# Four transposes moved from TensorE to SP's queue, half steps in two more blocks, and one tile's preparation moved ahead

## The chip, the core and the metric

The kernel runs on one core of one Trainium2 chip. The time is device microseconds of one execution of the whole program. Before the change it is 333.25 us, the median of 3 runs (333.15 to 333.43). Times on the trace are counted in us from the start of the profiled span.

## The reference

An attention with a linear kernel, followed by a gated feed-forward layer with a norm in front:

```python
# q, k, v: 8 batches, 8 heads, 576 rows, 64 columns
r = np.maximum(x, 0.0)                       # for q and k
phi = np.concatenate([r * c, r * s], axis=-1)   # c, s: cos and sin of the row's angle
kv = np.einsum('bhsf,bhsd->bhfd', k_p, v)
z = np.sum(k_p, axis=2)
num = np.einsum('bhsf,bhfd->bhsd', q_p, kv)
den = np.einsum('bhsf,bhf->bhs', q_p, z)[..., None] + 1e-06
x = (num / den)                              # as 4608 rows of 512
xn = x / np.sqrt(np.mean(x * x, axis=-1, keepdims=True) + 1e-06) * rms_g
g = xn @ w_gate                              # 512 x 1536
out = (g * (1.0 / (1.0 + np.exp(-g))) * (xn @ w_val)) @ w_out   # 1536 x 512
```

## The kernel before

**Batches, tiles, blocks.** A batch of 576 rows is cut into four tiles of 128 rows, (b, 0) to (b, 3), and a fifth of 64 rows; the fifths of two batches make one tile (b, 4). The four tiles of a batch are the four column groups of one block of the feed-forward layer, so blocks 0 to 7 belong to batches 0 to 7, and block 8 holds the four tiles of fifths.

**One tile's way into a block.** Features of q (q_feat, L222 on ScalarE, ACT, or L224 on VectorE, DVE) are transposed to rqT, over SP's DMA queue (q_turn, L293) or on TensorE, PE (q_turn_pe, L304, and a copy out of PSUM in q_evict, L312 on DVE or L314 on ACT). num_mm (L326) multiplies rqT with kvm into a PSUM tile "att". divide (L352, L355, L364, on DVE) makes x from it. sumsq (L375 on ACT) sums the squares, and the power of -0.5 is taken on GpSimd (L380). norm (L385 on DVE) makes xn, one of three buffers. xn is then transposed into its column group of the block's operand xnT in one of two ways: x_turn (L393), one DMA transpose of 128 x 512 on SP's queue straight into xnT; or x_turn_pe (L403), four PE transposes into a PSUM tile "xps", and x_evict, a copy from there into xnT (L409 on DVE, L411 on ACT).

**Steps.** Each of the nine blocks has 12 steps, numbered through from 0 to 107, so block 1 starts with step 12, block 2 with 24, block 3 with 36 and block 4 with 48. A step makes a tile gps of PSUM (x times w_gate), a tile vps (x times w_val), the silu of gps (sil, L657, ACT) and the product of vps and sil (hT, L666, DVE). From block 2 on, each step also runs four matmuls of the output layer of the block before (acc, L465), whose sums ACT copies to osb (L471) for the stores to out on SP (L455). Between blocks 0 and 1 stands lead(), which prepares batch 1 while the output layer of block 0 runs.

Blocks 0 to 4 start before all four column groups of their operand are ready. For them the table PARTS says which columns a step takes (gv_mm_part, L433): T[0] to T[3] are the single tiles of 128 columns, T[4] is the first half (tiles 0 and 1), T[5] the second half (tiles 2 and 3). A step of a single tile does four row groups n with 4 x 4 = 16 matmuls of 128 columns for gps and as many for vps; a step of a half does two with 8 matmuls of 256 columns each. From block 5 on, a step is 4 + 4 matmuls of 512 columns (L420).

**Order.** The order on each engine is the program's order. A plan written by hand, at(step, place, function, arguments), puts the preparation into the steps. In a step the places run as follows: "sp", "act0", "dve0"; then the DMA transposes that x_turn_late has put on a list; then the matmuls of gps; "mid" (in blocks with PARTS); those of vps; silu; "act1"; "act2"; "dve1"; hT; acc; "pe". So "mid" stands on PE between gps and vps, "dve1" on DVE ahead of the step's hT, and "act0" on ACT ahead of its silu. tile_at puts a tile into three steps, with its transpose on SP two steps after num_mm; pe_tile_at does the same with the transpose on PE.

**Buffers in PSUM.** gps, vps, xps and the transposes of q share one pool of three buffers (tag "gv"); which of the three a tile gets, and so which reader it waits for, is settled when the program is built. att has two buffers of its own, acc one.

Of the kernel before, what the change touches and what calls it, by code (L numbers as in the profile page):

```python
# [17 lines left out]
def kernel(  # L18
# [20 lines left out]
    NNT = DFF // P  # L39
# [439 lines left out]
    def at(g, w, f, *a):  # L479
        plan[g, w].append(lambda: f(*a))  # L480
# [6 lines left out]
    def tile_at(g, key, xblk, col):  # L487
        at(g, "pe", num_mm, key)
        at(g + 1, "dve0", divide, key)
        at(g + 1, "act1", sumsq, key)  # L490
        at(g + 2, "dve0", norm, key)
        at(g + 2, "sp", x_turn_late, key, xblk, col)
# [29 lines left out]
    at(1, "act0", q_evict, 0, 3)  # L522
    at(1, "mid", x_turn_pe, (0, 2))
    at(1, "dve1", x_evict, (0, 2), 0, 2, True)
    at(1, "pe", num_mm, (0, 3))
    at(2, "dve0", divide, (0, 3))
    at(2, "act1", sumsq, (0, 3))
    at(3, "dve0", norm, (0, 3))
    at(4, "mid", x_turn_pe, (0, 3))
    at(4, "dve1", x_evict, (0, 3), 0, 3, True)  # L530
    for c in range(2):
        at(2 + c, "act2", q_feat, 0, J, c, True)

# [8 lines left out]
    def pe_tile_at(g, key, xblk, col, gx, first="act1"):  # L542

        at(g, "pe", num_mm, key)
        at(g + 1, "dve0", divide, key)
        at(g + 1, "act1", sumsq, key)
        at(gx, "dve0", norm, key)
        at(gx, "pe", x_turn_pe, key)
        at(gx + 1, first, x_evict, key, xblk, col)

    def q2_at(g, b, t):
        for c in range(2):
            at(g, "act2" if c else "dve1", q_feat, b, t, c, c == 1)
        if t < J:
            at(g, "pe", q_turn, b, t)
# [4 lines left out]
    at(12, "pe", num_mm, (1, 3))  # L560
    at(13, "dve0", divide, (1, 3))
    at(13, "act1", sumsq, (1, 3))
    for t in (2, 3):
        at(12 + t, "dve0", norm, (1, t))
        at(12 + t, "pe", x_turn_pe, (1, t))
        at(13 + t, "act1", x_evict, (1, t), 1, t)
    q2_at(12, 1, J)


# [7 lines left out]
    for t, g in enumerate((13, 19, 20, 21, 23)):  # L577
        q2_at(g, 2, t)
    pe_tile_at(22, (2, 1), 2, 1, 24)
    pe_tile_at(24, (2, 2), 2, 2, 26)  # L580
    pe_tile_at(25, (2, 3), 2, 3, 27)


    at(15, "pe", load_q, 3)
# [35 lines left out]
    def run(g, w):  # L620
# [4 lines left out]
    T = [(c * P, P) for c in range(J)] + [(hf * HB, HB) for hf in range(2)]  # L625
    PARTS = {0: tuple((n,) + T[c] for n, c in (
        (0, 0), (0, 1), (0, 2), (4, 4), (6, 4), (0, 3), (4, 5), (6, 5), (8, 4), (10, 4), (8, 5),
        (10, 5),
    ))}
    for blk in (1, 2, 3, 4):  # L630
        PARTS[blk] = tuple(
            [(n,) + T[c] for c in range(2) for n in (0, 4, 8)]
            + [(n,) + T[5] for n in range(0, NNT, 2)]
        )

    def step(blk, nn):
        g = blk * NNT + nn
        run(g, "sp")
        run(g, "act0")
        run(g, "dve0")  # L640
        while late_turns:
            x_turn(*late_turns.pop(0))
        if nn == 0:
            hT[blk] = htp.tile([P, NNT, TB], BF16, name="hT", tag="hT")
        if blk in PARTS:
            n0, c0, cn = PARTS[blk][nn]
            ni = TB // cn
            gp = gv_mm_part(wg, "gps", blk, n0, c0, cn)
            run(g, "mid")
            vp = gv_mm_part(wv, "vps", blk, n0, c0, cn)  # L650
            dst = hT[blk][:, n0 : n0 + ni, c0 : c0 + cn]
        else:
            gp = gv_mm(wg, "gps", blk, nn)
            vp = gv_mm(wv, "vps", blk, nn)
            dst = hT[blk][:, nn, :]
        sil = silp.tile([P, TB], BF16, name="sil", tag="sil")
        K(nc.scalar.activation(out=sil[:, :], in_=gp[:, :], func=AF.Silu))  # L657
        run(g, "act1")
        ends = blk > 1 and nn % 3 == 2
        if not ends:  # L660
            run(g, "act2")
        run(g, "dve1")
        a, c = vp[:, :], sil[:, :]
        if blk in PARTS:
            a, c = (z.rearrange("p (i n) -> p i n", i=ni) for z in (a, c))
        K(nc.vector.tensor_tensor(out=dst, in0=a, in1=c, op=ALU.mult))  # L666
        if blk > 1:
            for i in range(4 * nn, 4 * nn + 4):
                out_mm(blk - 1, i)
        if ends:  # L670
            run(g, "act2")
        run(g, "pe")
# [165 lines left out]
```

## Time and profile before

| | before |
|---|---|
| median of 3 runs | 333.25 us |
| the profiled execution | 333.33 us |
| its span, first to last instruction | 331.2 us |
| PE busy, of the span | 320.0 us |
| clock granted to PE, mean | 0.998 of full |
| DMA transposes of rqT / xnT on SP | 32 / 24 |
| PE transposes of xn | 12 tiles of 4 |

How to read the rows: in a timeline a row has the start and the duration in us, the engine, the line, the operation with what it writes and reads (out<-in), its shape and how many of them were merged; square brackets hold the idle time of the engine ahead of it and what ended it. The ends of matmuls are modelled and overlap the next ones, so the distance from one row's start to the next is the time that counts. A row of waits has the total in us, how often, and the longest. SPq is the queue of DMAs that SyncE issues; the duration there is that of issuing, and the time to landing is counted from the start of the issue. A landing row gives the fastest, the median and the slowest of the transfers asked for.

### The profile page before, as it was taken

The page shows a single profiled execution, that of the slowest core. Times are in us where ns is not written, and L with a number is a line of the kernel's source. Part 1 is how long each engine was busy: PE and PEld are TensorE (multiplying, and loading weights), DVE is VectorE, ACT ScalarE, POOL GpSimd, SP SyncE. Part 2 cuts the span into 40 slices and gives each one's busy share as a digit, 9 for nine tenths or more (in the row PEclk, how much of TensorE's full clock was granted, in tenths as well). Part 3 has the DMA queues.
Part 4 walks back from the last instruction along what each step waited for, and adds up shares of the span by engine and source line. Part 5 has one row for each costly group of instructions (what it writes and reads, how often), then busy time and mean ns, then how long its engine had stood idle before and what let it go on. Part 6 is the DMA issues. An engine that isn't in the chain of part 4 may idle for free.

```text
span 331.2 us, 7596 instructions
## 1 busy us (share of the span) xinstructions
PE 320.0 (97%) x3048; PEld 214.2 (65%) x3048; DVE 189.6 (57%) x393; ACT 169.7 (51%) x322; POOL 43.2 (13%) x84
## 2 busy tenths in 40 slices
PE   6789999999999999999999999999999999999995
PEld 5568866999887788778877744554444444444443
DVE  4675476877956585687867676756543422223200
ACT  3765377767864366575646564644432322332221
POOL 3743343200101000011110001000100000000000
PEclk9999999999999999999999999999999999999999
DMA  7999999994148999999699995245124020000012
GB/s 218 303 207 207 290 337 385 360 180 95 35 97 228 353 247 281 201 313 149 162 221 245 214 239 131 70 93 111 48 67 109 32 65 33 32 34 32 32 64 96
DMA packets 78019, 54.76 MB, mean 165 GB/s; under 512 B 49024, under 2 KB 71312, under 8 KB 77984
## 3 DMA queue, kind: packets, MB, share of 16 engines
q1 hardware_dynamic: 70704, 39.99, 48.7%
q0 software_dynamic: 7120, 14.16, 16.7%
q8 instruction: 24, 0.39, 0.5%
q10 hardware_dynamic: 160, 0.13, 0.1%
q14 instruction: 11, 0.09, 0.1%
HBM read 38.01 MB, written 9.44 MB: 143 GB/s over the span
## 4 chain that ended last, share of the span: by engine, by line
PE 92%; ACT 2%; DMA 2%; DVE 1%; issue 1%; SPq 0%; ACTq 0%; DVEq 0%
PE acc L465 27%; PE gps L433 16%; PE vps L433 16%; PE vps L420 13%; PE gps L420 13%; PE att L326 3%; PE att L269 3%; DMA kbuf<-in_k_dram 2%; PE xps L403 1%; PE qtp L304 1%; ACT kp L222 1%; DMA out_dram<-osb 1%; DVE xn L385 0%; ACT qp L222 0%; ACT xnT L411 0%
## 5 line engine op out<-in xcount | busy, mean ns | idle before, releaser
L666 DVE TENSOR_TENSOR hT<-vps,sil 128x512 bf16<-128x512 f32 x108 | 74.6, 691 | 98.3 <-PE vps L420 62.0
L657 ACT ACTIVATE sil<-gps 128x512 bf16<-128x512 f32 x108 | 64.3, 596 | 99.5 <-PE gps L420 60.1
L465 PE MATMUL acc<-wo,hT 128*128 128x512 bf16 x420 | 105.7, 379 | 0.0
L465 PEld LDWEIGHTS <-hT 128*128 128x128 bf16 x420 | 40.1, 98 | 39.7
L433 PE MATMUL gps<-xnT,wg 128*128 128x128 bf16 (+1 forms) x704 | 62.7, 238 | 0.8 <-DVE xnT L409 0.5
L433 PE MATMUL vps<-xnT,wv 128*128 128x128 bf16 (+1 forms) x704 | 62.8, 238 | 0.6 <-ACT sil L657 0.5
L433 PEld LDWEIGHTS <-wg 128*128 128x128 bf16 x704 | 50.3, 98 | 7.1 <-issue 0.8
L433 PEld LDWEIGHTS <-wv 128*128 128x128 bf16 x704 | 51.2, 98 | 3.8 <-issue 0.6
L380 POOL TENSOR_TENSOR rs<-ss,mhalf 128x1 f32<-128x1 f32 x36 | 20.4, 566 | 200.3 <-ACT sq L375 200.3
L420 PE MATMUL vps<-xnT,wv 128*128 128x512 bf16 x144 | 37.0, 379 | 0.0
L420 PE MATMUL gps<-xnT,wg 128*128 128x512 bf16 x144 | 36.9, 379 | 0.0
L471 ACT COPY osb<-acc 128x512 f32<-128x512 f32 x35 | 20.4, 584 | 31.5 <-PE acc L465 31.5
L420 PEld LDWEIGHTS <-wv 128*128 128x128 bf16 x192 | 18.8, 98 | 22.6
L385 DVE SCALAR_TENSOR_TENSOR xn<-x,rs,gb 128x512 bf16<-128x512 f32 x36 | 27.0, 749 | 7.9 <-POOL rs L380 7.6
L420 PEld LDWEIGHTS <-wg 128*128 128x128 bf16 x192 | 18.0, 98 | 20.1
L375 ACT ACTIVATE sq<-x 128x513 f32<-128x513 f32 x36 | 22.6, 628 | 7.6 <-DVE x L364 7.2
L364 DVE TENSOR_TENSOR x<-att,rec 128x512 f32<-128x512 f32 x36 | 24.9, 691 | 1.2
L224 DVE TENSOR_SCALAR kp<-kbuf,trig 128x512 bf16<-128x512 f32 x50 | 22.6, 483 | 3.5 <-DMA kbuf<-in_k_dram 3.1
L224 DVE TENSOR_SCALAR qp<-qbuf,trig 128x512 bf16<-128x512 f32 x50 | 22.9, 479 | 0.0
L222 ACT ACTIVATE kp<-kbuf,trig 128x512 bf16<-128x512 f32 x30 | 20.7, 714 | 2.8 <-DMA kbuf<-in_k_dram 2.8
L222 ACT ACTIVATE qp<-qbuf,trig 128x512 bf16<-128x512 f32 x30 | 21.1, 713 | 0.2 <-DMA qbuf<-in_q_dram 0.2
L326 PEld LDWEIGHTS <-rqT 128*128 128x128 bf16 x320 | 14.4, 98 | 7.9 <-DVE rqT L312 0.9
(64 smaller groups left out, 189.2 us busy)
## 6 DMA issues: line engine op xcount, KB each, us to landing
out_dram<-osb SPq DMA_DIRECT2D x70, 128.0 KB, 2.1
kbuf<-in_k_dram SPq DMA_DIRECT2D x5, 640.0 KB, 6.0
vbuf<-in_v_dram SPq DMA_DIRECT2D x5, 640.0 KB, 7.2
qbuf<-in_q_dram SPq DMA_DIRECT2D x5, 640.0 KB, 7.4
kbuf<-in_k_dram SPq DMA_DIRECT2D x5, 512.0 KB, 4.8
vbuf<-in_v_dram SPq DMA_DIRECT2D x5, 512.0 KB, 5.8
qbuf<-in_q_dram SPq DMA_DIRECT2D x5, 512.0 KB, 6.1
kbuf<-in_k_dram POOLq DMA_DIRECT2D x3, 640.0 KB, 10.4
```

Source lines behind the costliest of these rows:

```text
L222: K(nc.scalar.activation(out=dst, in_=src, func=AF.Relu, scale=scale))
L224: K(nc.vector.tensor_scalar(out=dst, in0=src, scalar1=scale, scalar2=0.0, op0=ALU.mult, op1=ALU.max,))
L326: K(nc.tensor.matmul(nums[key][:, h // Z, (h % Z) * E : (h % Z) * E + D + 1], lhsT=rqT[a, t][:, h, :], rhs=kvm[a % NK][:, h, 0 : D + 1], s ...
L364: K(nc.vector.tensor_tensor(out=x[:, 0:DM].rearrange("p (z s d) -> p z s d", z=2, d=D), in0=a[:, :, :, 0:D], in1=r.unsqueeze(3).to_broadca ...
L375: K(nc.scalar.activation(out=sq[:, :], in_=xs[key][:, :], func=AF.Square, scale=1.0 / math.sqrt(DM), accum_out=ss[:, :],))
L380: K(nc.gpsimd.tensor_tensor(out=rs[:, :], in0=ss[:, :], in1=mhalf[:, :], op=ALU.pow))
L385: K(nc.vector.scalar_tensor_tensor(out=xn[:, :], in0=xs.pop(key)[:, 0:DM], scalar=rss.pop(key)[:, :], in1=gb[:, :], op0=ALU.mult, op1=ALU. ...
L420: K(nc.tensor.matmul(ps[:, :], lhsT=w[:, dt, nn * P : (nn + 1) * P], rhs=xnT[blk][:, dt, :], start=(dt == 0), stop=(dt == NDT - 1),))
L433: K(nc.tensor.matmul(ps[:, i * cn : (i + 1) * cn], lhsT=w[:, dt, (n0 + i) * P : (n0 + i + 1) * P], rhs=xnT[blk][:, dt, c0 : c0 + cn], star ...
L465: K(nc.tensor.matmul(acc[blk][:, :], lhsT=hT[blk][:, nn, jt * P : (jt + 1) * P], rhs=wo[:, nn, :], start=(nn == 0), stop=(nn == NNT - 1),))
L657: K(nc.scalar.activation(out=sil[:, :], in_=gp[:, :], func=AF.Silu))
L666: K(nc.vector.tensor_tensor(out=dst, in0=a, in1=c, op=ALU.mult))
```

## The change

```diff
     at(1, "act0", q_evict, 0, 3)
     at(1, "mid", x_turn_pe, (0, 2))
     at(1, "dve1", x_evict, (0, 2), 0, 2, True)
-    at(1, "pe", num_mm, (0, 3))
-    at(2, "dve0", divide, (0, 3))
-    at(2, "act1", sumsq, (0, 3))
+    at(1, "mid", num_mm, (0, 3))
+    at(1, "dve1", divide, (0, 3))
+    at(2, "act0", sumsq, (0, 3))
     at(3, "dve0", norm, (0, 3))
-    at(4, "mid", x_turn_pe, (0, 3))
-    at(4, "dve1", x_evict, (0, 3), 0, 3, True)
+    at(3, "pe", x_turn_pe, (0, 3))
+    at(4, "dve0", x_evict, (0, 3), 0, 3, True)
...
-    for t in (2, 3):
-        at(12 + t, "dve0", norm, (1, t))
-        at(12 + t, "pe", x_turn_pe, (1, t))
-        at(13 + t, "act1", x_evict, (1, t), 1, t)
+    for t, g in ((2, 13), (3, 15)):
+        at(g, "dve0", norm, (1, t))
+        at(g, "sp", x_turn_late, (1, t), 1, t)
...
-    pe_tile_at(24, (2, 2), 2, 2, 26)
-    pe_tile_at(25, (2, 3), 2, 3, 27)
+    for t in (2, 3):
+        tile_at(22 + t, (2, t), 2, t)
...
     for blk in (1, 2, 3, 4):
-        PARTS[blk] = tuple(
-            [(n,) + T[c] for c in range(2) for n in (0, 4, 8)]
-            + [(n,) + T[5] for n in range(0, NNT, 2)]
-        )
+        head = (
+            [(n,) + T[c] for c in range(2) for n in (0, 4, 8)] if blk < 3
+            else [(n,) + T[4] for n in range(0, NNT, 2)]
+        )
+        PARTS[blk] = tuple(head + [(n,) + T[5] for n in range(0, NNT, 2)])
```

In block 0 the fourth tile's num_mm goes from the end of step 1 to between gps and vps of that step, its division ahead of hT of step 1, its sum of squares ahead of the silu of step 2, its PE transposes from between gps and vps of step 4 to the end of step 3, and the copy out of PSUM ahead of that of hT of step 4. Tiles (1, 2), (1, 3), (2, 2) and (2, 3) are transposed by one DMA each on SP's queue; their 16 PE transposes and 4 ACT copies go. The norm of (1, 2) is one step earlier, in step 13; that of (1, 3) stays in step 15, and those of batch 2 in steps 26 and 27. In blocks 3 and 4, the first six steps take tiles 0 and 1 together, 256 columns at a time, so tile 1 is wanted in the first step of the block and no longer in the fourth.

## Prediction

> **What bounds the kernel now.** I read the page first, then who waited for whom, then TensorE (PE) in order of time.
>
> ```profile
> span 331.2 us, 7596 instructions
> PE 320.0 (97%) x3048; PEld 214.2 (65%) x3048; DVE 189.6 (57%) x393; ACT 169.7 (51%) x322; POOL 43.2 (13%) x84
> PE 92%; ACT 2%; DMA 2%; DVE 1%; issue 1%; SPq 0%; ACTq 0%; DVEq 0%
> PE vps L433 <- ACT sil L657: 0.5, 1, 0.5
> ```
>
> PE is busy for 97% of the span and carries 92% of the chain that ended last. An edit therefore counts in one of three ways: it takes instructions off PE, it removes a wait of PE, or it gives PE a new one. The last row is such a wait, once, 0.5 us. PE has only nine kinds of waits in all, none longer than 0.6 us behind its start, so a shift is not swallowed further on: gains and losses add up.
>
> **Fourth tile of the first batch (block 0).** The wait lies in step 4:
>
> ```profile
> 28.55 1.04 PE L433 MATMUL gps<-xnT,wg 128*128 128x256 bf16 x8
> 29.42 0.39 PE L403 MATMUL xps<-ident_b,xn 128*128 128x128 bf16 x4
> 30.33 1.03 PE L433 MATMUL vps<-xnT,wv 128*128 128x256 bf16 x8 [0.52 <-ACT sil L657]
> 29.68 0.60 ACT L657 ACTIVATE sil<-gps 128x512 bf16<-128x512 f32 x1 [0.40 <-PE gps L433]
> ```
>
> Three PSUM buffers are shared by gps, vps and the transposes' xps. Here vps got the buffer of its own step's gps and had to wait until the silu (29.68 to 30.28) had read it. Without that it would have followed the four transposes, which cost 0.22 (rows below), at 29.65: 0.68 us lost. In the changed program as built, the transposes stand at the end of step 3 and step 4's vps waits for the hT product of step 3 instead. What has to be in time for that:
>
> ```profile
> 22.60 1.02 ACT L314 COPY rqT<-qtp 128x1024 bf16<-128x1024 bf16 x1
> 23.86 1.06 PE L433 MATMUL vps<-xnT,wv 128*128 128x128 bf16 x16
> 26.06 0.69 DVE L364 TENSOR_TENSOR x<-att,rec 128x512 f32<-128x512 f32 x1
> 26.85 0.63 ACT L375 ACTIVATE sq<-x 128x513 f32<-128x513 f32 x1
> 28.25 0.75 DVE L385 SCALAR_TENSOR_TENSOR xn<-x,rs,gb 128x512 bf16<-128x512 f32 x1 [0.49 <-POOL rs L380]
> ```
>
> The num matmuls now stand where vps stood (23.86), and their operand is there at 23.62, so they do not wait. The division goes ahead of hT of step 1 and ends near 25.5 instead of 26.75 (estimate); the sum of squares goes ahead of the silu of step 2, near 25.6. From sum to norm took 28.25 - 26.85 = 1.40, so the norm could start at 27.0; VectorE (DVE) is then in hT of step 2 and the norm follows at about 27.7, ending at 28.4, just before PE wants it at 28.55. The silu and hT that are pushed back have over 0.3 us of room. Gain between 0 (norm late, the wait merely moves) and 0.68; I take 0.68, because each row leaves it room.
>
> **Two tiles of block 1 (steps 13 to 18).**
>
> ```profile
> 62.70 1.06 PE L433 MATMUL gps<-xnT,wg 128*128 128x128 bf16 x16
> 64.48 0.39 PE L403 MATMUL xps<-ident_b,xn 128*128 128x128 bf16 x4
> 64.70 1.06 PE L433 MATMUL gps<-xnT,wg 128*128 128x128 bf16 x16
> 65.60 1.06 PE L433 MATMUL vps<-xnT,wv 128*128 128x128 bf16 x16
> 66.49 0.39 PE L403 MATMUL xps<-ident_b,xn 128*128 128x128 bf16 x4
> 66.92 1.05 PE L433 MATMUL gps<-xnT,wg 128*128 128x128 bf16 x16
> 70.49 1.04 PE L433 MATMUL gps<-xnT,wg 128*128 128x256 bf16 x8
> 64.01 0.57 ACT L657 ACTIVATE sil<-gps 128x512 bf16<-128x512 f32 x1
> 65.80 0.60 ACT L657 ACTIVATE sil<-gps 128x512 bf16<-128x512 f32 x1 [0.60 <-PE gps L433]
> ```
>
> Four transposes hold PE for 64.70 - 64.48 = 0.22 us; the second set costs 0.43, since the step behind it also waits 0.21 for a copy. From 62.70 (step 14) to 70.49 (step 18) are 7.79 us: four steps of 1.79, plus 0.22, plus 0.43. That 0.65 goes. But without the transposes the PSUM buffers fall differently. In the changed program as built, gps of step 15 waits for the silu of step 14, and vps of step 15 for the silu of its own step: block 0's wait moves here. The first silu ends at 64.58, so gps starts at 64.63 instead of 64.48: 0.15. Then gps runs 0.90, its silu starts 0.20 behind it (65.80 against 65.60), takes 0.60, and vps follows 0.05 later: 0.85 lost. Steps 14 to 17 take 7.16 + 1.00 = 8.16, 0.37 more than before, and step 18 wants its operand at 70.86, less the 0.68 of block 0: 70.18.
>
> Now the transposes as transfers. SP issues xnT of (1,2), then rqT of batch 2, then xnT of (1,3), then q of batch 3. Queued behind them are only rqT, wanted in step 19, and q, wanted from step 24.
>
> ```profile
> 63.57 0.74 DVE L385 SCALAR_TENSOR_TENSOR xn<-x,rs,gb 128x512 bf16<-128x512 f32 x1
> 65.36 0.74 DVE L385 SCALAR_TENSOR_TENSOR xn<-x,rs,gb 128x512 bf16<-128x512 f32 x1
> 64.13 1.34 SPq L293 DMA_TRANSPOSE rqT<-qp  x1
> DMA to landing us min/median/max: 6.3/6.3/6.3
> DMA to landing us min/median/max: 2.4/3.8/7.6
> ```
>
> The first landing row is this rqT alone, the second all 24 transfers of L393. The norm of (1,2) moves from 63.57 to the end of the division before it, ahead of hT of step 13; that hT is then about 0.7 later and is wanted only by gps of step 16. The norm of (1,3) stays in step 15 and ends at 65.36 + 0.74, less 0.68, at 65.42; SP is free by then, so this transfer starts at 65.45. Fastest (2.4) it lands at 67.85, and PE does not wait; slowest (7.6) at 73.05, and PE waits 2.9. The nearest row is the rqT directly ahead of it on the queue: it landed at 70.43 in the old trace, with the loads of batch 3 in flight. For transposes close behind each other:
>
> ```profile
> 146.26 1.63 SPq L293 DMA_TRANSPOSE rqT<-qp  x1
> 147.98 1.26 SPq L393 DMA_TRANSPOSE xnT<-xn  x1
> DMA to landing us min/median/max: 6.1/6.1/6.1
> DMA to landing us min/median/max: 4.8/4.8/4.8
> ```
>
> These land at 152.36 and 152.78, 0.42 apart. So I take 70.43 + 0.4 = 70.8 and a wait of 0.6 us at step 18. The Trainium skill, page "DMA: Bandwidth & Descriptors", section "Queues, rings and completion order", has each DMA engine consume one queue's descriptors in ring order; the 0.42 between these two landings agrees.
>
> The Trainium skill, page "VectorE: DVE Perf Modes", section "Rules for kernel authors", speaks against this part: TensorE for a 128x128 transpose where PSUM will do, the DMA crossbar otherwise. By the 390 ns of its section "The three transpose paths", the four removed sets would be worth an estimated 6.2 us of PE instead of 0.9; the trace has 0.22 a set, and the rows decide.
>
> **Two tiles of block 2.** Their transposes leave the ends of steps 26 and 27: 2 x 0.22 = 0.44. Built, the order of buffers brings no own-step wait here. The transfers are issued in steps 26 and 27 and wanted in step 30.
>
> ```profile
> 93.07 0.75 DVE L385 SCALAR_TENSOR_TENSOR xn<-x,rs,gb 128x512 bf16<-128x512 f32 x1 [0.17 <-POOL rs L380]
> 101.75 1.04 PE L433 MATMUL gps<-xnT,wg 128*128 128x256 bf16 x8
> ```
>
> The second tile's norm ends at 93.82; step 30 starts 7.9 later, 7.5 without the transposes. Between them on SP stand two stores of out, and behind them two rqT that are wanted in steps 32 and 34. At 3.8 the wait is nothing, at 7.6 with the stores ahead about 1; I take nothing. The four ScalarE copies that go are on no chain of PE, save the 0.21 counted above.
>
> **Half steps in blocks 3 and 4.** Twelve steps go from 2 x 16 matmuls of 128 columns to 2 x 8 of 256.
>
> ```profile
> 32.98 1.04 PE L433 MATMUL gps<-xnT,wg 128*128 128x256 bf16 x8
> 43.46 1.89 PE L465 MATMUL acc<-wo,hT 128*128 128x512 bf16 x8
> 118.17 1.06 PE L433 MATMUL gps<-xnT,wg 128*128 128x128 bf16 x16
> 119.96 1.03 PE L465 MATMUL acc<-wo,hT 128*128 128x512 bf16 x4
> 108.39 2.45 SPq L393 DMA_TRANSPOSE xnT<-xn  x1
> DMA to landing us min/median/max: 6.9/6.9/6.9
> 153.52 1.06 PE L433 MATMUL gps<-xnT,wg 128*128 128x128 bf16 x16
> ```
>
> Twelve runs of 8 fill 32.98 to 43.46, 0.873 each; two runs of 16 fill 118.17 to 119.96, 0.895 each. So 24 x 0.022 = 0.53 us. The price: the second tile of each block is now wanted in its first step, not its fourth. For block 3 it lands at 108.39 + 6.9 = 115.3 and is wanted at 118.17. For block 4 it lands at 152.78 and is wanted at 153.52, 0.74 of cover; both ends are set by PE's steps and move together. Nothing, then; with 7.6 instead of 4.8 it would be 2.1.
>
> **Sum.** 0.68 - 0.37 - 0.6 + 0.44 + 0.53 = 0.68 us off. The profiled execution took 333.33 (its span 331.2 and 2.1 around it), 0.08 over the median of 333.25; so 332.65 and 332.57. Forecast 332.6.
>
> **Rivals.**
> B, the transfer is hidden: (1,3) lands within 4.7 us of its issue, so step 18 does not wait. For it: the median of 3.8, and q now queues behind it. Against it: the 6.3 of its neighbour. Gain 1.28: 332.0. The Trainium skill, page "Advanced Engine Details and Errata", section "X-Bar Transpose (TRN2)", calls transpose DMAs as fast as regular ones, and by that rule B would hold; here the same kind of transfer took 2.4 to 7.6.
> C, slower: three transposes among plain loads make (1,3) land late. All gains are gone at 6.0 us from issue, and at 7.6 the net is 1.6 lost: 334.8; between the two about 334.2. For it: 6.9 and 7.6 do occur beside loads. Against it: the median of 3.8, and that q's loads now start behind it. It is slower by more than 0.2% from 6.7 us on.
> D, the second tile of block 4 is late in step 48, by 2.1 at most: 334.6. Against it: the cover of 0.74.
> E, it does not do what it says: the norm of the fourth tile is late, and the 0.68 is not won: 333.2.
>
> **How the numbers follow.** Forecast 0.40, B 0.28, C 0.20, D 0.07, E 0.05. A measurement of this kernel can tell about 0.2% (0.67 us) from no change; the forecast sits on that bound and gives half of its chance to each side. Faster: 0.20 + 0.28 = 0.48. Slower: 0.14 of C and 0.06 of D, 0.20. Within: 0.32. Range 331.9 (B, a little under) to 334.4 (C up to a wait of 2.4); the likeliest case alone is 332.0 to 333.1.
>
> **What would show it.** Step 4's vps starts as gps ends; a wait for sil of about 0.85 stands before vps in step 15; a wait for xnT stands before gps in step 18, 0 to 1.2; the runs of x16 in blocks 3 and 4 are gone, 0.02 a run; no transposes at the ends of steps 14, 15, 26, 27. Wrong would be: no wait in step 15, over 1.3 in step 18, any wait in step 30, 36 or 48.

## The result and the profile after

The changed kernel takes 332.82 us (median of 22 runs, 332.6 to 333.21), the kernel before 333.39 (22 runs beside them, 333.06 to 333.69). The ratio is 0.9985, with a 95% interval of 0.9978 to 0.9991: 0.57 us off between the medians, where 0.68 was forecast. The interval leaves out 1, so the gain is clear of the noise of these runs; it is under the 0.2% (0.67 us) that the prediction set as its bound, and by that bound it falls under no change. The profiled execution took 332.82 with a span of 330.7.

The page of the changed kernel, its span and the busy times of the engines:

```profile
span 330.7 us, 7188 instructions
PE 319.5 (97%) x2840; PEld 211.1 (64%) x2840; DVE 189.5 (57%) x393; ACT 167.8 (51%) x318; POOL 42.8 (13%) x84
```

From the view of who waited for whom, the waits of PE that are new or have moved (total, times, longest):

```profile
PE vps L433 <- ACT sil L657: 0.7, 1, 0.7
...
PE gps L433 <- DMA xnT<-xn: 0.5, 1, 0.5
...
PE acc L465 <- ACT osb L471: 0.2, 1, 0.2
```

PE issues 208 fewer matmuls (3048 to 2840). Sixteen of them are the transposes; the other 192 come from the half steps, where one matmul of 256 columns takes the place of two of 128 and saves only 0.02 us a run of 8. The three waits are where gains went: one for a silu (0.5 us, in another place, before), one for a DMA transpose, and one for a copy to osb.

Where they stand, on PE's timeline (start, duration, idle before and its cause). Steps 3 and 4 of block 0 first, then steps 12 and 14 to 18 of block 1:

```profile
28.47 0.39 PE L403 MATMUL xps<-ident_b,xn 128*128 128x128 bf16 x4
28.69 1.04 PE L433 MATMUL gps<-xnT,wg 128*128 128x256 bf16 x8
29.56 1.04 PE L433 MATMUL vps<-xnT,wv 128*128 128x256 bf16 x8
...
58.20 1.05 PE L433 MATMUL gps<-xnT,wg 128*128 128x128 bf16 x16
...
62.03 1.06 PE L433 MATMUL gps<-xnT,wg 128*128 128x128 bf16 x16
62.92 1.06 PE L433 MATMUL vps<-xnT,wv 128*128 128x128 bf16 x16
63.97 1.05 PE L433 MATMUL gps<-xnT,wg 128*128 128x128 bf16 x16
65.71 1.05 PE L433 MATMUL vps<-xnT,wv 128*128 128x128 bf16 x16 [0.69 <-ACT sil L657]
...
69.28 1.06 PE L433 MATMUL vps<-xnT,wv 128*128 128x128 bf16 x16
70.83 0.93 PE L433 MATMUL gps<-xnT,wg 128*128 128x256 bf16 x7 [0.50 <-DMA xnT<-xn]
```

In step 4 vps now follows gps at once. In step 15 it does not: from 63.97 a free vps would start 0.89 later, at 64.86, and it starts at 65.71, so 0.85 us are lost although the bracket shows 0.69 (the ends of matmuls are modelled). In step 18 gps would start at 69.28 + 0.89 = 70.17 and starts at 70.83: 0.66 lost. The DMAs behind the last row, on SP's queue:

```profile
62.67 1.30 SPq L393 DMA_TRANSPOSE xnT<-xn  x1
64.16 1.23 SPq L293 DMA_TRANSPOSE rqT<-qp  x1
65.48 1.73 SPq L393 DMA_TRANSPOSE xnT<-xn  x1
67.31 2.28 SPq L93 DMA_DIRECT2D qbuf<-in_q_dram  x2
```

And the time from issue to landing, fastest, median and slowest, first of the two xnT, then of the rqT between them:

```profile
DMA to landing us min/median/max: 5.2/5.2/5.2
DMA to landing us min/median/max: 6.0/6.0/6.0
```

So the three land at 67.9, 70.16 and 70.68, and PE goes on 0.15 us after the last.

How each stretch of the program changed, from the start of gps in the steps named (us; a row for each kernel of the experiments too, so that they can be compared later; "less" is its median minus that of the kernel before run beside it):

| kernel | 12 to 18 | 24 to 30 | 36 to 42 | 48 to 54 | median | less |
|---|---|---|---|---|---|---|
| before | 11.62 | 18.77 | 17.17 | 17.09 | 333.39 | |
| after | 12.63 | 18.31 | 16.93 | 17.02 | 332.82 | -0.57 |
| e1, without block 1's part | 11.62 | 18.31 | 16.93 | 17.02 | 331.77 | -1.53 |
| e2, buffers in strict turn | 12.85 | 18.32 | 16.93 | 17.02 | 332.76 | -0.54 |
| e3, rqT later | 11.97 | 18.31 | 16.93 | 17.01 | 332.60 | -0.70 |
| e4, v later, not held | 15.23 | 18.32 | 16.93 | 17.01 | 336.81 | +3.51 |
| e5, block 0 alone | 11.62 | 18.77 | 17.17 | 17.08 | 332.56 | -0.68 |
| e6, block 2 alone | 11.63 | 18.31 | 17.17 | 18.09 | 332.56 | -0.68 |
| e7, half steps alone | 11.62 | 18.76 | 16.93 | 17.01 | 332.99 | -0.25 |
| e8, v held back | 11.06 | 18.31 | 16.93 | 17.01 | 331.25 | -1.99 |
| e9, osb first | 12.45 | 18.32 | 16.92 | 16.68 | 332.48 | -0.73 |
| e10, osb first, in before | 11.62 | 18.77 | 17.17 | 16.92 | 332.98 | -0.23 |
| e11, e1 with v held back | 11.62 | 18.31 | 16.93 | 17.01 | 331.68 | -1.53 |
| e12, e8 and e9 | 10.97 | 18.32 | 16.93 | 16.68 | 330.90 | -2.31 |

Where no landing sets them, the stretches repeat to 0.01 us when the code in them is the same. Where one does, they do not: 12 to 18 took 12.63 in the changed kernel and 12.45 in e9, and 48 to 54 of e6 has a late transpose in it. The medians of the kernel before lie between 333.21 and 333.39 from one group of runs to the next. So a part of 0.1 to 0.3 us is read from its stretch, and the total only says whether it reached the end.

### The profile page after: what moved, and what is told of

Same layout as the page of the kernel before. It is cut to its first block, busy times and chain, and to the rows that moved or that the text cites. A ratio compares the mean times of both kernels' runs of the same rounds, so it can differ in the third digit from the quotient of the medians.

```text
span 330.7 us, 7188 instructions
## 1 busy us (share of the span) xinstructions
PE 319.5 (97%) x2840; PEld 211.1 (64%) x2840; DVE 189.5 (57%) x393; ACT 167.8 (51%) x318; POOL 42.8 (13%) x84
## 4 chain that ended last, share of the span: by engine, by line
PE 87%; DVE 4%; DMA 3%; ACT 2%; issue 2%; SPq 0%; POOL 0%; ACTq 0%; DVEq 0%
PE acc L465 26%; PE gps L433 14%; PE vps L433 14%; PE gps L420 13%; PE vps L420 13%; PE att L326 3%; PE att L269 3%; DMA kbuf<-in_k_dram 2%; DMA xnT<-xn 2%; DVE xn L385 1%; PE acc L799 1%; PE qtp L304 1%; ACT kp L222 1%; PE xps L403 1%; DVE x L364 1%
## 5 line engine op out<-in xcount | busy, mean ns | idle before, releaser
L433 PE MATMUL gps<-xnT,wg 128*128 128x256 bf16 (+1 forms) x608 | 62.4, 250 | 1.2 <-DVE xnT L409 0.5
L433 PE MATMUL vps<-xnT,wv 128*128 128x256 bf16 (+1 forms) x608 | 62.5, 250 | 0.7 <-ACT sil L657 0.7
L433 PEld LDWEIGHTS <-wg 128*128 128x128 bf16 x608 | 48.0, 98 | 8.8 <-issue 1.3
L433 PEld LDWEIGHTS <-wv 128*128 128x128 bf16 x608 | 49.4, 98 | 5.1 <-issue 0.8
L420 PEld LDWEIGHTS <-wv 128*128 128x128 bf16 x192 | 18.8, 98 | 22.7
L420 PEld LDWEIGHTS <-wg 128*128 128x128 bf16 x192 | 18.0, 98 | 20.1
```

Of the source, the lines that this page charges most:

```text
L420: K(nc.tensor.matmul(ps[:, :], lhsT=w[:, dt, nn * P : (nn + 1) * P], rhs=xnT[blk][:, dt, :], start=(dt == 0), stop=(dt == NDT - 1),))
L433: K(nc.tensor.matmul(ps[:, i * cn : (i + 1) * cn], lhsT=w[:, dt, (n0 + i) * P : (n0 + i + 1) * P], rhs=xnT[blk][:, dt, c0 : c0 + cn], star ...
```

## The experiments

**Block 1's part taken out (e1).** The four matmuls that turn a tile on PE come back for (1, 2) and (1, 3); the rest of the change stays.

```diff
-    for t, g in ((2, 13), (3, 15)):
-        at(g, "dve0", norm, (1, t))
-        at(g, "sp", x_turn_late, (1, t), 1, t)
+    for t in (2, 3):
+        at(12 + t, "dve0", norm, (1, t))
+        at(12 + t, "pe", x_turn_pe, (1, t))
+        at(13 + t, "act1", x_evict, (1, t), 1, t)
```

> The changed kernel with tiles (1,2) and (1,3) transposed on PE again, as before the change; the other parts stay. Theory (block 1 gives back what the rest wins): steps 12 to 17 take 11.62 us again as before instead of 12.63, no wait of 0.7 in front of vps of step 15, no wait for xnT in step 18; about 1.0 us faster than the changed kernel, 331.8, and 1.5 faster than the kernel before. Rival (the two waits in block 1 are made up for further on, or the other parts are worth less than counted): within 0.3 us of the changed kernel, 332.5 to 333.1.

Measured 331.77 us (331.68 to 332.28), ratio 0.9954 (0.9941 to 0.9966). Steps 12 to 18 are back at 11.62. So two of the four tiles moved to SP's queue, block 1's, cost 1.0 us net, and the change without them is better than either kernel.

**Which of the two waits sets step 18 (e2)?** In place of one pool of three PSUM buffers, three pools of one, handed out in strict turn, so that vps of step 15 doesn't get the buffer of its own gps.

```diff
-    ps_gv = ctx.enter_context(tc.tile_pool(name="psgv", bufs=3, space=bass.MemoryType.PSUM))
+    ps_gvs = [
+        ctx.enter_context(tc.tile_pool(name=f"psgv{u}", bufs=1, space=bass.MemoryType.PSUM))
+        for u in range(3)
+    ]
...
+            return ps_gvs[gv_n[0] % 3].tile(shape, dtype, name=name, tag=tag)
```

> The changed kernel with the three PSUM buffers given out in strict turn, so that vps of step 15 no longer waits for the silu of its own step. Theory (the landing of xnT of (1,3) paces step 18): the wait in step 15 goes, the transfer still lands near 70.7, and the wait in front of gps of step 18 grows from 0.5 to about 1.5; the time stays within 0.2 us of the changed kernel's 332.8. Rival (the wait in step 15 is the price, the landing follows PE): 0.9 to 1.0 us faster, 331.8 to 331.9.

Measured 332.76 us (332.5 to 332.99), ratio 0.9985 (0.9976 to 0.9993). Steps 15 and 18 on its PE timeline (the lines are ten further down here):

```profile
63.71 1.06 PE L443 MATMUL gps<-xnT,wg 128*128 128x128 bf16 x16
64.60 1.06 PE L443 MATMUL vps<-xnT,wv 128*128 128x128 bf16 x16
...
70.95 0.82 PE L443 MATMUL gps<-xnT,wg 128*128 128x256 bf16 x6 [1.72 <-DMA xnT<-xn]
```

The wait in step 15 is gone, and all of it has reappeared in front of step 18: PE gets there at 69.07 instead of 70.17 and starts at 70.95, 0.12 later than in the changed kernel. xnT(1, 3), issued at 65.39, took 5.4 us and landed at 70.8: its landing sets step 18. In the changed kernel the 0.85 us lost to the silu added nothing to that, since step 18 would have waited that much longer.

**Is the transpose ahead of it on the queue the reason (e3)?** The rqT of (2, 0) is issued three steps later, in step 16, behind xnT(1, 3).

```diff
-    for t, g in enumerate((13, 19, 20, 21, 23)):
+    for c in range(2):
+        at(13, "act2" if c else "dve1", q_feat, 2, 0, c, c == 1)
+    at(16, "pe", q_turn, 2, 0)
+    for t, g in enumerate((19, 20, 21, 23), 1):
```

> The changed kernel with the DMA transpose of rqT (2,0) issued in step 16 instead of step 13, so that xnT of (1,3) stands directly behind xnT of (1,2) on SP's queue. Theory (the transposes go in the order of the queue): xnT of (1,3) lands 0.5 to 1.5 us earlier, 69.2 to 70.2, the wait in step 18 falls from 0.5 to 0 to 0.1; 332.2 to 332.4. Rival (the loads of v of batch 3 on the other queue decide when any transpose lands): it lands at 70.5 or later, no change, 332.8.

Measured 332.6 us (332.06 to 333.27), ratio 0.9979 (0.9969 to 0.9989): the mechanism as expected, the time not. xnT(1, 3), issued at 65.5, landed 4.2 us later, at 69.7 instead of 70.68, and step 18 did not wait; steps 12 to 18 took 11.97 us, with the wait in step 15 still there. But rqT, issued at 68.71, was late instead, for num_mm of step 19:

```profile
70.23 1.04 PE L433 MATMUL gps<-xnT,wg 128*128 128x256 bf16 x8
...
75.75 0.43 PE L326 MATMUL att<-kvm,rqT 128*128 128x65 bf16 x8 [0.59 <-DMA rqT<-qp]
```

A loss of 0.66 in step 18 became one of 0.76 here (75.75 against 74.12 + 0.87; the bracket shows 0.59). The order on the queue counts: without the rqT ahead of it xnT(1, 3) landed 1.0 us earlier, with the loads as before. Why rqT was late is not told apart: it was issued three steps later, and the load of q had gone onto SP's queue at 66.81, ahead of it.

**Loads in flight, first try: later, but not held (e4).** The load of v of batch 3 leaves lead() and is put at the end of step 16.

```diff
+    at(16, "pe", load_v, 3)
...
         load_k(3)
-        load_v(3)
```

> The changed kernel with the loads of v of batch 3 issued in step 16 instead of in the lead before block 1. As built, vps of step 15 then does not wait for the silu of its own step either. If the loads in flight delay the transposes: xnT of (1,3) lands within 4 us of its issue, before 69.5, and with both waits gone the time is 331.2 to 331.8. If the queue's order alone decides: it lands near 70.7, the wait in step 18 grows to about 1.5 and the time stays at 332.8.

Measured 336.81 us (334.52 to 337.32), ratio 1.0087 (1.0061 to 1.0113). Both theories missed, and the trace tells why. GpSimd waits for nothing in that place, so it issued the load as soon as its power for (1, 3) was done. The timeline of GpSimd, and PE's step 18:

```profile
62.89 0.55 POOL L380 TENSOR_TENSOR rs<-ss,mhalf 128x1 f32<-128x1 f32 x1 [1.76 <-ACT sq L375]
63.40 1.41 POOL L93 DMA_DIRECT2D vbuf<-in_v_dram  x2
```
```profile
73.42 0.88 PE L433 MATMUL gps<-xnT,wg 128*128 128x256 bf16 x6 [4.09 <-DMA xnT<-xn]
```

The load was moved from 56.93 to 63.40, right on top of the transposes. xnT(1, 2), issued at 62.66 ahead of it, now landed in 2.5 us instead of 5.2; rqT, behind it, in 8.6 instead of 6.0, and xnT(1, 3) in 7.8 instead of 5.2. (That wait for its own silu in step 15 is gone here too; it could not help.) A step in the plan is a place in an engine's order, not a time; as an edit this run failed, but it shows that a load on the other queue moves the landings: the transpose ahead of it was faster, the two behind it slower.

**Loads in flight, held back (e8).** GpSimd first copies one element of hT of step 17, and so cannot issue the load before that is there.

```diff
+    def v3_gated():
+        pool_after(hT[1][0:1, 8, P : P + 1])
+        load_v(3)
...
+    at(17, "pe", v3_gated)
...
         load_k(3)
-        load_v(3)
```

> The changed kernel with the load of v of batch 3 held back: GpSimd first copies one element of hT of step 17, then issues the load (about 71 us), so that no load is in flight while the transposes of 62 to 66 us are. Theory (loads on the other queue set the landing): rqT(2,0) and xnT(1,3) land within 3 us of their issue, no wait for xnT ahead of step 18; vps of step 15 gets another buffer here and doesn't wait for its own silu either; steps 12 to 18 take 11.0 us instead of 12.63, total 331.2 us, 331.0 to 331.6, ratio 0.9935. Rival 1 (the transposes take 5 us for themselves or by their order on the queue): xnT(1,3) lands 5 us after 65.5, step 18 waits 1.4 us, 332.8. Rival 2: v arrives too late for its cast in step 22 (81 us), which shows as a wait there for vbuf; 332 or more although step 18 did not wait.

Measured 331.25 us (331.06 to 331.78), ratio 0.9941 (0.9928 to 0.9953). GpSimd, SP and PE on its timeline:

```profile
70.08 0.31 POOL L216 COPY probe<-hT 1x1 bf16<-1x1 bf16 x1 [6.75 <-DVE hT L671]
70.33 1.41 POOL L93 DMA_DIRECT2D vbuf<-in_v_dram  x2
```
```profile
62.54 1.31 SPq L393 DMA_TRANSPOSE xnT<-xn  x1
64.03 1.23 SPq L293 DMA_TRANSPOSE rqT<-qp  x1
65.36 2.13 SPq L393 DMA_TRANSPOSE xnT<-xn  x1
```
```profile
63.69 1.06 PE L433 MATMUL gps<-xnT,wg 128*128 128x128 bf16 x16
64.58 1.06 PE L433 MATMUL vps<-xnT,wv 128*128 128x128 bf16 x16
...
68.16 1.06 PE L433 MATMUL vps<-xnT,wv 128*128 128x128 bf16 x16
69.14 1.03 PE L433 MATMUL gps<-xnT,wg 128*128 128x256 bf16 x8
```

The landings, again of the two xnT and then of the rqT between them:

```profile
DMA to landing us min/median/max: 2.5/3.1/3.6
DMA to landing us min/median/max: 4.6/4.6/4.6
```

The same three transposes, issued 0.13 earlier, landed in 2.5, 4.6 and 3.6 us (the second and third later than the 3 us expected), and the two waits are gone: step 18 starts at 69.14 where PE is free at 69.05. Steps 12 to 18 take 11.06 us, 0.56 less than with the transposes on PE. The third lands at 68.96, so there is no room left to speak of. The load of q, issued at 67.58, is behind them here as it is in the changed kernel (67.31), so q is not what made the difference. The wait in step 15 went because vps got another of the three buffers in this build. The two repairs can be told apart roughly by other runs: with the wait in step 15 gone and the load in flight (e2) steps 12 to 18 took 12.85; with the landing in time and the wait still there (e3) 11.97; with both here 11.06. On PE they took 11.62, so neither repair alone makes the move pay. The held load with the wait in step 15 kept was not run.

**The same, with block 1 on PE (e11).** This is the control: does holding back the load help by itself?

> Block 1's two tiles on PE as before (the rest of the change kept), with the load of v of batch 3 held back behind hT of step 17 as in the run at 331.25. Theory (holding the load matters only through the landings of the transposes): 331.7 to 331.9 as without holding it (331.77), steps 12 to 18 in 11.6 us. Rival (the held load helps by itself, or the DMAs of the weights): 331.3 or less.

Measured 331.68 us (331.62 to 332.26), ratio 0.9956 (0.9944 to 0.9967), beside 331.77 without the hold. It does not. The same edit of block 1 thus costs 1.0 us as first built (after against e1) and wins 0.4 to 0.6 with the load held back and the other buffer for vps of step 15 (e8 against e11: 0.43 by the medians, 0.56 by the stretch).

**The other three parts alone (e5, e6, e7).** Each is the kernel before with one part of the change's diff.

> Only block 0's part of the change (the fourth tile of the first batch one step ahead), the rest as before. Theory: the wait of vps for its own silu in step 4 goes, step 12 starts 0.67 us earlier (58.2 instead of 58.87), all behind it follows unchanged: 332.7 us beside 333.39 before, ratio 0.998. Rival (E of the prediction): what block 0 wins is given back at a later wait, 333.2 to 333.4, and step 18, 24 or 36 starts where it started before.

Measured 332.56 us (332.34 to 332.86) beside 333.24, ratio 0.9972 (0.9959 to 0.9985). Step 12 starts at 58.10, and nothing behind it takes the gain back.

> Only block 2's part (tiles (2,2) and (2,3) turned over SP's queue), the rest as before. Theory: the eight PE transposes and the waits at their copies go from steps 26 to 29, 0.44 to 0.46 us, with both landings ahead of step 30: 332.9 to 333.0 us, ratio 0.9987. Rival: something ahead of step 36 takes it back, 333.3 to 333.4.

Measured 332.56 us (332.4 to 333.65) beside 333.24, ratio 0.9978 (0.9969 to 0.9987). Steps 24 to 30 win 0.46 as expected; the total wins a little more, 0.68. Where the other 0.2 are from is open: the start of block 0, behind the loads of the weights, differs by as much between executions (step 0 to 5 took 11.36 in this profiled one and 11.51 in that of before, with the same code). The profiled execution was the longest of its eleven, and shows what a late transpose costs elsewhere, in step 54:

```profile
170.94 1.05 PE L433 MATMUL gps<-xnT,wg 128*128 128x256 bf16 x8 [0.83 <-DMA xnT<-xn]
```

The transfer issued at 162.78 took 8.1 us there, behind a load of q issued 1.5 us ahead of it; the same transfer in the old trace, as close behind that load, took 6.7 and was in time.

> Only the half steps in blocks 3 and 4, the rest as before. By the prediction's term 0.53 us: 332.85. By the profile of the changed kernel 0.24 in block 3 and 0.07 in block 4, because acc of step 51 waits longer for the copy to osb: 333.1, ratio 0.9991, with about 0.3 us of idle PE ahead of acc in step 51.

Measured 332.99 us (332.75 to 333.24) beside 333.24, ratio 0.9992 (0.9983 to 1.0), at the edge of what can be told. The stretches have 0.24 in block 3 and 0.08 in block 4: the sizes of the changed kernel's profile and not the prediction's 0.53.

**Why block 4 wins less (e9, e10).** In the changed kernel the view by time has ACT, DVE and PE so, around the end of step 50:

```profile
159.96 0.60 ACT L657 ACTIVATE sil<-gps 128x512 bf16<-128x512 f32 x1 [0.74 <-PE gps L433]
162.33 0.63 ACT L375 ACTIVATE sq<-x 128x513 f32<-128x513 f32 x1 [1.78 <-DVE x L364]
...
162.96 0.57 ACT L471 COPY osb<-acc 128x512 f32<-128x512 f32 x1
```
```profile
160.44 0.74 DVE L385 SCALAR_TENSOR_TENSOR xn<-x,rs,gb 128x512 bf16<-128x512 f32 x1
...
161.53 0.69 DVE L364 TENSOR_TENSOR x<-att,rec 128x512 f32<-128x512 f32 x1
```
```profile
160.63 1.03 PE L465 MATMUL acc<-wo,hT 128*128 128x512 bf16 x4
...
162.37 1.04 PE L433 MATMUL vps<-xnT,wv 128*128 128x256 bf16 x8
163.58 1.02 PE L465 MATMUL acc<-wo,hT 128*128 128x512 bf16 x4 [0.18 <-ACT osb L471]
```

The four matmuls that finish acc start at 160.63, and PE is on to gps of step 51 at 161.49. The copy out of acc could start about then. But on ACT it stands behind the sum of squares of (5, 0), and that waits 1.78 us for DVE, which is at work without a break. So the copy starts at 162.96, and acc of step 51, which has only one buffer, waits: 163.58 instead of 162.37 + 0.87 = 163.24, 0.34 lost. In the kernel before, the rows of DVE and ACT lie 0.36 later (xn at 160.80, the copy at 163.32) and vps of step 51 lies 0.50 later (162.87); acc started at 163.94 there, 0.18 after vps was through. Counted from the start of step 48 (153.15 here, 153.52 before) DVE's xn came at 7.29 and 7.28: DVE sets the time of the copy and got no earlier with the half steps, so what PE won in steps 48 to 51 went into the wait ahead of acc. The test moves that one sum of squares behind the copy:

```diff
-        at(g + 1, "act1", sumsq, key)
+        at(g + 1, "act2" if key == (5, 0) else "act1", sumsq, key)
```

> The changed kernel with one sumsq moved: that of tile (5,0) in step 50 goes on ACT from ahead of the copy to osb to behind it. Theory (block 4's half steps won only 0.07 us because the copy stands on ACT behind a sumsq that waits for DVE's x of step 50, whose time DVE sets and not PE): the copy starts as acc of step 50 ends (161.6 instead of 162.96), acc of step 51 doesn't wait (0.34 us from vps's end before), steps 48 to 54 take 16.68 instead of 17.02, total 332.5 beside 332.82. Rival: DVE is the bound of these steps, the next thing on PE waits instead, steps 48 to 54 stay at 17.0 and the total at 332.8.

> The kernel before with the same one move of sumsq of (5,0). Theory: acc of step 51 waits 0.18 us there, so steps 48 to 54 take 16.91 instead of 17.09 and the total is 333.06 beside 333.24. With the run above this prices block 4's half steps without the wait: 16.91 - 16.68 = 0.23, as block 3's 0.24. Rival: no move, 17.09.

Measured 332.48 us (332.21 to 332.85), ratio 0.9976 (0.9966 to 0.9985), in the changed kernel, and 332.98 (332.75 to 334.42), ratio 0.9998 (0.9987 to 1.0009), in the one before. The second total cannot be told from no change, but the stretches can: 16.68 and 16.92, both to 0.01 as expected. ACT and PE in the first:

```profile
161.45 0.59 ACT L471 COPY osb<-acc 128x512 f32<-128x512 f32 x1 [1.14 <-PE acc L465]
162.09 0.63 ACT L375 ACTIVATE sq<-x 128x513 f32<-128x513 f32 x1
```
```profile
162.12 1.04 PE L433 MATMUL vps<-xnT,wv 128*128 128x256 bf16 x8
163.00 1.03 PE L465 MATMUL acc<-wo,hT 128*128 128x512 bf16 x4
```

With the copy first, half steps in block 4 win 16.92 - 16.68 = 0.24, as in block 3.

**Both repairs (e12).**

> The changed kernel with v of batch 3 held back and with sumsq of (5,0) behind the copy to osb. Theory: the two gains add, 331.25 - 0.34 = 330.9 us, ratio 0.993; steps 12 to 18 in 11.06, 48 to 54 in 16.68. Rival: a transpose of (4,2) or (4,3), wanted in step 54, comes late once the steps ahead are shorter: a wait for xnT ahead of step 54, 331.2.

Measured 330.9 us (330.65 to 334.16), ratio 0.9939 (0.9921 to 0.9957): the best of all, 2.31 under the kernel before. The profiled execution was the longest of its eleven; in it step 0 starts at 21.54 instead of 19.6 and block 0 takes longer, and from step 12 on the stretches are those expected or a little less (10.97 and 16.68). No transpose was late ahead of step 54.

## Why the prediction was right, and where a size was off

- **Block 0, 0.68.** Right: 58.20 against 58.87 at step 12, 0.68 between the medians of e5 and of the kernel before. The norm ran from 27.60 to 28.34, forecast 27.7 to 28.4.
- **Block 1, steps 14 to 17, -0.37.** Right: from 62.03 to 70.17 are 8.14 us, forecast 8.16, with 0.85 for the own silu and 0.16 for gps of step 15 (63.97 - 62.92 - 0.89). But e2 shows that this term and the next were not two losses: had the wait in step 15 not been there, step 18 would have waited that much longer. Their sum, 1.0, was the landing's to set, and so it was right to add them only because the wait at step 18 was worked out from when PE would want the tile.
- **Step 18, -0.6.** The size came out, 0.66, but in part by luck. The landing was taken as 70.8 from the rqT of the old trace and a distance of 0.42, and was 70.68. The prediction moved the time at which PE wants the tile 0.68 earlier and left the landing of rqT where it was in the old trace, without a reason; moved along, it would have given no wait. In fact rqT could not be issued earlier, because xnT(1, 2) now stood ahead of it on SP (62.67 + 1.30), although its last features were there at 63.43: it was issued at 64.16, and at 64.13 before, and landed at 70.16. The distance held: 0.5, also in e4 (72.8 and 73.3), and 0.3 in e8 (68.63 and 68.96). What sets the landing the prediction named only in passing, as loads in flight. The runs show two things: the rqT ahead on the queue (5.2 us from issue to landing, 4.2 without it in e3) and the load of v (3.6 without it in e8).
- **Block 2, +0.44.** Right: 0.46, with landings of 2.4 and 3.4 us and no wait in step 30.
- **Half steps, +0.53.** The mis-sized term: 0.24 + 0.07 = 0.31 in the changed kernel. A run was priced rightly (0.24 a block where nothing else stands in the way, 12 x 0.022 = 0.26 forecast), and the cover for block 4's second tile held. What was missed is that acc of step 51 was already waiting 0.18 us in the trace of before, for a copy whose time DVE sets through ACT's order. It stood in no row of waits there, only in the distance of two starts on PE, and what was taken from PE ahead of it went into that wait. The premise that failed is the one the prediction opens with: that the nine kinds of waits in the list are all that PE has, so that no shift is swallowed further on.
- **The sum.** 0.67 - 1.01 + 0.46 + 0.31 = 0.43 in the profiled execution, whose last stretches start 0.44 earlier (step 60 at 187.84 instead of 188.28); 0.57 between the medians, against 0.68. The 0.13 between the two is of the size by which the medians of the kernel before differ from group to group (333.21 to 333.39), so the terms account for 0.43 and not for 0.57.

Of the rivals, B (no wait at step 18, 332.0) needed a landing within 4.7 us; it was 5.2. With the load of v held (e8) it was 3.6, and with rqT behind it (e3) 4.2: step 18 then does not wait, as B says. C (late, slower) did not happen in the changed kernel, but e4 has it: 7.8 us from issue, and a kernel slower by 0.9%. D and E did not happen.

The Trainium skill's page "Advanced Engine Details and Errata", section "X-Bar Transpose (TRN2)", has transpose DMAs as fast as regular ones. Here one transfer of 128 x 512, xnT(1, 2), took 2.5 us in e8 and 5.2 in the changed kernel. The plain stores of 128 KB on the same queue took 2.1 us in the median of the changed kernel and 5.0 to 8.2 among the loads, issued between 55 and 60 us. Plain DMAs take longer there too, so the prediction's step from this rule to B does not follow: the rule does not tell when a tile is there. No run here compares the two kinds alone. The rule weighed in the prediction, "VectorE: DVE Perf Modes", section "Rules for kernel authors", to turn on TensorE where PSUM will do, held for block 1 as first built (e1 against after), did not in e8 (11.06 us for steps 12 to 18, 11.62 in e11), and did not in block 2, where the move to the DMA queue won 0.46.

## What to carry to other kernels

A transpose moved from a full engine to a DMA queue is paid for in landing time, and that depended here on what another queue had in flight and on the transposes ahead on its own: look at the loads on the timeline of DMAs, and hold one back with a real dependency, not with a later place in the order. Look also at which buffers the new build hands out, since a move can bring a wait of its own (1.0 us in step 15 here). Price a shorter PE stretch only up to the next thing on PE that another engine's order sets; compare the distance of starts with the length of the work, since a wait that is not in the list of waits can already be there. When two waits follow each other on an engine, find out which one sets the end before removing the first.

## What the runs showed of the hardware

That the loads on GpSimd's queue slow the transposes on SP's that much was not expected. The view of DMAs has a row of rates in 40 slices of the window and one for GpSimd's queue (q0: packets, MB, share of 16 engines' time). In the changed kernel, 62 to 72 us, and in the kernel with v held back, 62 to 70:

```profile
GB/s 311 365 340 369 369 418 467 369 414 365 414 403 370 297 320 168 159 82 86 39 84 288 234 292 335 269 101 29 7 13 9 87 360 205 356 344 344 360 257 215
...
q0 software_dynamic: 281, 1.14, 29.7%
```
```profile
GB/s 220 205 128 118 61 77 41 61 10 148 220 212 75 0 0 0 151 220 209 211 278 170 115 6 0 6 9 10 10 236 288 129 0 0 0 82 72 72 133 164
...
q0 software_dynamic: 16, 0.05, 1.9%
```

The view of DMAs lists the two halves of the load of v in the changed kernel, with their sizes and the us from issue to landing:

```profile
vbuf<-in_v_dram POOLq DMA_DIRECT2D x1, 640.0 KB, 9.9
...
vbuf<-in_v_dram POOLq DMA_DIRECT2D x1, 512.0 KB, 8.6
```

The half of 512 KB was issued first, at 56.93, that of 640 KB at 57.62, both behind the load of k, so they landed at 65.5 and 67.5. GpSimd's queue moved 1.14 MB in the first window and 0.05 in the second. With the load in flight the DMA engines move 297 to 467 GB/s until about 65.7 us (15 slices of 0.25), and the transposes issued from 62.67 on land at 67.9 to 70.7; with it held, they land at 65.0 to 69.0. The Trainium skill, page "DMA: Bandwidth & Descriptors", section "Queues, rings and completion order", has each DMA engine take turns between the queues that have work, a packet at a time. That xnT(1, 2) took about twice as long beside the load (5.2 against 2.5 us) agrees with it; how the packets were interleaved no run here shows.
